# Sums of log decays by channel, made on TensorE for the first four units of an RWKV-7 and MLP kernel

## The chip, the cores and the metric

The kernel runs on one core of one Trainium2 chip. The metric is the device time of one execution in microseconds (us). A profiled execution has a time of its own, and its trace gives the span from the first to the last instruction; the time shown for the kernel is the median of several executions without profile.

## The reference

The program is an RWKV-7 attention block (batch 4, 8 heads, 768 steps, head width 40) followed by an MLP with a sigmoid-approximated GELU (3072 tokens, 320 to 2048 to 320). Everything is fp32.

```python
for t in range(S):                                   # S = 768
    y[:, :, t] = einsum('bhd,bhde->bhe', r_t, state)
    Sa = einsum('bhde,bhe->bhd', state, a_t)
    state = state * w_t[:, :, None, :] - einsum('bhd,bhe->bhde', Sa, b_t) + einsum('bhd,bhe->bhde', v_t, k_t)
x = y.transpose(0, 2, 1, 3).reshape(B * S, H * D)
h = x @ w_in
out = (h / (1 + exp(-1.702 * h))) @ w_out
```

The decay `w` lies between 0.85 and 0.95, per batch, head, step and channel. A blocked form of the recurrence needs products of `w` over steps, that is exponentials of sums of `log w`.

## The kernel before, in words

**Units.** The 768 steps are cut into 12 chunks of 64 steps. A unit is one chunk of two of the four batch entries, so there are 24 units, numbered i = 2c + p for chunk c and pair of batch entries p. Units of one pair follow each other in c, because the state is handed on. An MLP chunk c can start when units 2c and 2c+1 are finished.

**One unit.** `decay(i)` makes decay factors, `prep(i)` multiplies a, b, k by them and makes score matrices (`ps_A`, `ps_RV`), `inverse(i)` inverts triangular 64 x 64 systems by an iteration of five levels, and `solve(i)` makes the output and the next state. One level is: matmuls (`ps_level`), a copy of the result (`W`, line 651), a subtraction from two times the identity (`E`, line 653), a 32 x 32 block transposition (`ES`, line 615) and a masked spread of it (`EX`, line 620 on ScalarE, 622 on VectorE or GpSimd), which the next level's matmuls need. The unit's result `x` (line 814) is written to DRAM and read back transposed as `xT` (lines 824 and 828), for the MLP.

**The decay factors.** Two forms are needed.
- By time: steps on the partitions, channels on the free axis. `logw` (128 x 320, 160 KB, from `in_w`) is loaded, its logarithm taken in place (line 478), and `by_time` multiplies it by the constant matrix `incl` of 0, 1 and -1 on TensorE (`ps_cum`), which gives running sums measured from the middle of the chunk (MID = 32). `G` is their exponential (line 514).
- By channel: channels on the partitions, steps on the free axis. This is a second copy of `w`, laid out by the host: `wc` (128 x 528, 264 KB, from `in_wc`). Its logarithm is taken (line 477), and two scans on VectorE (lines 485 and 486) make the running sums, backwards from the middle for the first 32 steps and forwards for the others. `FT` (line 506) and `GT` (line 507), each 128 x 512, are their exponentials with plus and minus sign; `wch` (lines 509 and 510) holds the chunk's end values.

`FT` and `GT` scale a, k and b: the products `ak<-ak,FT` (line 541), `b<-b,GT` (543) and `ak<-ak,GT` (546) stand at the head of every unit's chain.

**Order.** Nothing in the program's text orders the engines. Each piece of work is a task in `Plan`, with a rank, a cost for every engine that may run it, what it reads and writes, how many buffers its outputs have, and if it uses PSUM, one of four pairs of banks. `Plan.order` runs a greedy list schedule with these costs: whenever an engine is free, it takes the able task of lowest rank. The order found is then emitted, and at run time each engine works through its own list and waits on semaphores. So any change of a task's cost can change the order of everything behind it. A task whose `engines` names several (for instance `EX`: POOL, DVE or ACT) goes to whichever is free first in that plan. DMA tasks stand in SyncE's list, and all DMAs are issued from SyncE's queue. The tasks that concern the change are

```python
def load_w(i):
    for name, of, src, n in (("wc", wc_of, wc_d, 528), ("logw", logw_of, w_d, DM)):
        plan.add(-2 if i == 2 else 10 * i - 30, {"SP": 350.0}, ...)
```

`logarithm(i)` and `decay(i)`. The functions `prep`, `inverse` and `solve` of a unit follow from its rank.

**The weights.** `w_in` and `w_out` arrive as eight pieces of 128 x 1280 64-bit numbers (1280 KB each). Each piece is turned into fp32 in `weight(n, ...)`: one ScalarE instruction (line 408) and five on VectorE (lines 412, 416, 417, 420 and 424; the sum of line 424 finishes the piece). Pieces 0 to 3 are `w_in`, which `ps_up` needs; pieces 4 to 7 are `w_out`, which `ps_down` needs. The MLP's matmuls have the highest rank numbers (10000 and up), so they fill TensorE where attention leaves it free.

**ScalarE's tables.** Logarithm and exponential share one table, the GELU has another. For the first four units (EARLY = 4) no GELU runs yet, and the exponentials stand without a table load before them.

Of the kernel before, what the change touches and what calls it, by code (L numbers as in the profile page):

```python
# [22 lines left out]
ALU = mybir.AluOpType  # L23
ACT = mybir.ActivationFunctionType
# [201 lines left out]
def rwkv7_gelu_quick(ctx: ExitStack, tc: tile.TileContext, time_d, v_d, w_d, wc_d, ak_d, b_d, rv_d, w_in, w_out, out):  # L226
    nc = tc.nc
    H, D, S = 8, 40, out.shape[0] // 4
    DM = H * D
    C = 64  # L230
    MID = C // 2
# [6 lines left out]
    LEVELS = 5  # L238
    WALK = "ebufbub"
    EARLY = 4  # L240
    ROUNDS, WINDOW, SHARE = 4, 5000.0, 1.0
    RANKS = [14, 16, 20, 24, 35, 37, 39, 41]
    HALF = [slice(0, 64), slice(64, 128)]
    BITS = (0, 1)
    QUARTERS = [(0, 0), (1, 1), (0, 1), (1, 0)]
# [7 lines left out]
    plan = Plan(dict(logw=3, wc=3, G=1, wch=3, wz=2, time=2, ak=2, b=2, rv=2, FT=3, GT=1, kh=2, bh=2, zr=2, rz=2,  # L253
                     A=1, B=1, RV=2, E0=2, W0=2, P21=2, W=2, E=2, ES=2, EX=2, T=2, Tc=1, QT=1, zraw=2, zT=1, M=2, x=1, xT=3, g=4, ob=1), 4)
    tiles, psums, drams = {}, {}, {}

    def single(name, shape):
        return const.tile(shape, FP32, tag=name, name=name)

    def buf(name, n, shape, dt=FP32):  # L260

        if (name, n) not in tiles:
            s = n % plan.slots[name]
            tiles[name, n] = work.tile(shape, dt, tag=f"{name}{s}", name=name)
        return tiles[name, n]

    def psum(t, name):
        if t.pair not in psums:
            psums[t.pair] = banks.tile([128, 2, 512], FP32, tag=f"pair{t.bank}", name=name)
        return psums[t.pair]  # L270

    def mm(o, lhsT, rhs, start):
        nc.tensor.matmul(o, lhsT, rhs, start=start, stop=True, skip_group_check=True)  # L273

    def head(e, f, b, u):
        return e + 2 * f + 4 * (b ^ u)


    def pe(*sets):

        return {"PE": sum(n * 2 * max(58.0, cols / 1.2 + 3) for n, cols in sets), "instr": sum(16 * n for n, _ in sets)}
# [13 lines left out]
    def of(e):  # L295
        return nc.gpsimd if e == "POOL" else nc.vector


    def several(name, shape):
        return [single(f"{name}{i}", shape) for i in range(plan.slots[name])]  # L300
# [18 lines left out]
    def select(t, compare, base, sign, fill):  # L319

        nc.gpsimd.affine_select(out=t, in_=t, compare_op=compare, fill=fill, base=base,
                                pattern=[[sign, t.shape[-1]]], channel_multiplier=-sign)


    incl = single("incl", [128, 64])
    nc.gpsimd.memset(incl, 1.0)
    for p in HALF:
        q = slice(p.start, p.start + MID)
        nc.gpsimd.memset(incl[q], 0.0)
        select(incl[q], ALU.is_ge, 0, 1, -1.0)  # L330
        select(incl[p.start + MID:p.stop], ALU.is_ge, -MID, 1, 0.0)

    starts = single("starts", [128, 8, 33])
    nc.gpsimd.memset(starts, 1.0)
# [106 lines left out]
    ak_of, b_of, rv_of = lambda i: ak_t[i % 2], lambda i: b_t[i % 2], lambda i: rv_t[i % 2]  # L441

    RV_of = lambda i: buf("RV", i, [128, 13, 8, 8])
    logw_of = lambda i: buf("logw", i, [128, DM])

    wc_of = lambda i: buf("wc", i, [128, 2, 8 * 33])

    def load_w(i):
        for name, of, src, n in (("wc", wc_of, wc_d, 528), ("logw", logw_of, w_d, DM)):
            plan.add(-2 if i == 2 else 10 * i - 30, {"SP": 350.0}, lambda t, of=of, src=src: nc.sync.dma_start(of(i), src[i]),  # L450
                     writes=[(name, i)], size=128 * n * 4)

# [14 lines left out]
    FT_of = lambda i: buf("FT", i, [128, 8, 64])  # L467
    GT_of = lambda i: buf("GT", i, [128, 8, 64])
    wch_of = lambda i: buf("wch", i, [128, 2, 8])
# [4 lines left out]

    def logarithm(i):
        def go(t):
            nc.scalar.activation(wc_of(i), wc_of(i), ACT.Ln)
            nc.scalar.activation(logw_of(i), logw_of(i), ACT.Ln)
        plan.add(10 * i - 30, {"ACT": 1080.0 + (1300.0 if i >= EARLY + 2 else 0.0)}, go,
                 reads=[("logw", i), ("wc", i)] + ([("exps", i - 2)] if i > 1 else []), writes=[("log", i)])  # L480

        def sums(t):

            wc, one = wc_of(i), starts.rearrange("p h t -> p (h t)")
            nc.vector.tensor_tensor_scan(wc[:, 0, ::-1], one, wc[:, 0, ::-1], 0.0, ALU.mult, ALU.subtract)
            nc.vector.tensor_tensor_scan(wc[:, 1], one, wc[:, 1], 0.0, ALU.mult, ALU.add)
        plan.add(10 * i - 12, {"DVE": 1400.0, "sbuf": True}, sums, reads=[("log", i)], uses=[("wc", i)], writes=[("sums", i)])

    def decay(i):
        T = lambda *names: [(n, i) for n in names]  # L490
        R = 10 * i - 9

        def by_time(t):
            ps, lw = psum(t, "ps_cum"), logw_of(i)
            for n in (1, 0):
                for b in BITS:
                    u = b ^ n
                    mm(ps[HALF[u], b, :160], incl[HALF[b]], lw[HALF[b], n * 160:(n + 1) * 160], True)
        plan.add(R, pe((1, 160)), by_time, reads=T("log"), uses=T("logw"), room=T("G"), writes=T("cum"), pair=("cum", i))

        def exp_channel(t):
            if i >= EARLY:
                nc.scalar.preload_act_table_set("natural_log_exp_and_others")
            sums = wc_of(i).rearrange("p n (h t) -> p n h t", t=33)
            by_half = lambda t: t.rearrange("p h (n t) -> p n h t", n=2)
            nc.scalar.activation(by_half(FT_of(i)), sums[:, :, :, :32], ACT.Exp)
            nc.scalar.activation(by_half(GT_of(i)), sums[:, :, :, 1:], ACT.Exp, scale=-1.0)

            nc.scalar.activation(wch_of(i)[:, 0], sums[:, 0, :, 0], ACT.Exp, scale=-1.0)
            nc.scalar.activation(wch_of(i)[:, 1], sums[:, 1, :, 32], ACT.Exp)  # L510

        plan.add(R, {"ACT": 1600.0 + (1300.0 if i >= EARLY else 0.0)}, exp_channel, reads=T("cum", "sums"), uses=T("wc"),
                 writes=T("FT", "GT", "wch"))
        plan.add(R, {"ACT": 460.0}, lambda t: nc.scalar.activation(G_of(i), psum(t, "")[:, :, :160], ACT.Exp, scale=-1.0),
                 reads=T("FT"), writes=T("G", "exps"), pair=("cum", i))
        if i >= 2:
            plan.add(R, {"DVE": 180.0, "POOL": 200.0}, lambda t: of(t.engine).tensor_mul(
                wz_of(i), wch_of(i)[:, 0], wch_of(i - 2)[:, 1]),
                     reads=T("wch") + [("wch", i - 2)], writes=T("wz"))
# [367 lines left out]
    for i in range(3):  # L887
        load_w(i)
    for i in range(2):
        logarithm(i)  # L890
# [3 lines left out]
    for i in range(NU):  # L894
        decay(i)
        if i + 3 < NU:
            load_w(i + 3)
        if i + 2 < NU:
            logarithm(i + 2)
        if i >= 2:  # L900
            load(i)
        prep(i)
        inverse(i)
        solve(i)
        if i % 2:
            mlp(i // 2)
# [88 lines left out]
```

## Time and profile before

| | before |
|---|---|
| median of 3 executions | 743.05 us (742.98 to 743.25) |
| the profiled execution's own time | 743.23 us |
| its span in the trace | 741.2 us (2.03 us lie outside it) |
| mean granted TensorE clock | 0.969 |
| busy: PE, PEld, VectorE (DVE), ScalarE (ACT), GpSimd (POOL) | 672.6, 539.6, 445.1, 372.8, 223.3 us |
| DMA traffic | 70.86 MB |

PE is TensorE's matmuls, PEld its weight loads, which lie beside them. The engines' busy shares are means over the whole span, and this kernel has two stages with different limits: at the start no MLP work is there, and from about 75 us on there is. A row of the profile names the line, the engine, the operation, and the tile written and the tiles read (`wc<-starts,wc`), with the number of instructions behind an x. All matmuls have line 273 or 272, that of the helper `mm`, and are told apart by their tiles. An fp32 matmul appears as two passes, each with its weight load. "issue" is time for which the trace shows no reason.

### The profile page before, as it was taken

The page shows a single profiled execution, that of the slowest core. Times are in us where ns is not written, and L with a number is a line of the kernel's source. Part 1 is how long each engine was busy: PE and PEld are TensorE (multiplying, and loading weights), DVE is VectorE, ACT ScalarE, POOL GpSimd, SP SyncE. Part 2 cuts the span into 40 slices and gives each one's busy share as a digit, 9 for nine tenths or more (in the row PEclk, how much of TensorE's full clock was granted, in tenths as well). Part 3 has the DMA queues.
Part 4 walks back from the last instruction along what each step waited for, and adds up shares of the span by engine and source line. Part 5 has one row for each costly group of instructions (what it writes and reads, how often), then busy time and mean ns, then how long its engine had stood idle before and what let it go on. Part 6 is the DMA issues. An engine that isn't in the chain of part 4 may idle for free.

```text
span 741.2 us, 43007 instructions
## 1 busy us (share of the span) xinstructions
PE 672.6 (91%) x19968; PEld 539.6 (73%) x19968; DVE 445.1 (60%) x783; ACT 372.8 (50%) x693; POOL 223.3 (30%) x279
## 2 busy tenths in 40 slices
PE   3464896898998999999999999999999999999997
PEld 2364674686776776988778889888678877987564
DVE  6889897876567556666766656666547556421000
ACT  4764664358447439545544544745845444342120
POOL 7554244242304331233332522322332433100000
PEclk9678997999999999999999999999999999999999
DMA  7964361242323332242332332341331220111000
GB/s 226 356 203 132 132 226 42 85 122 82 101 55 99 105 85 87 75 138 71 108 94 71 107 101 63 98 135 45 100 101 48 76 84 21 31 47 30 12 11 19
DMA packets 32434, 70.86 MB, mean 96 GB/s; under 512 B 5120, under 2 KB 14336, under 8 KB 31232
## 3 DMA queue, kind: packets, MB, share of 16 engines
q1 hardware_dynamic: 32256, 68.11, 30.1%
q8 instruction: 157, 2.57, 1.5%
q14 instruction: 21, 0.17, 0.1%
HBM read 60.23 MB, written 7.86 MB: 92 GB/s over the span
## 4 chain that ended last, share of the span: by engine, by line
PE 77%; ACT 10%; DVE 7%; DMA 2%; issue 2%; POOL 1%; DVEq 0%; ACTq 0%; POOLq 0%; SPq 0%
PE ps_down L273 27%; PE ps_up L273 23%; PE ps_level L273 7%; PE ps_y L273 4%; PE ps_B L273 4%; PE ps_X L273 2%; ACT L849 2%; ACT g L849 2%; PE ps_Q L273 1%; ACT EX L620 1%; PE ps_zT L273 1%; DVE ES L615 1%; PE ps_T L273 1%; PE ps_rz L273 1%; PE ps_N L273 1%
## 5 line engine op out<-in xcount | busy, mean ns | idle before, releaser
L273 PE MATMUL ps_up<-xT,w_sb 64*64 64x256 f32 x3840 | 250.0, 380 | 5.1 <-ACT g L849 4.4
L273 PE MATMUL ps_down<-w_sb,g 64*64 64x320 f32 x3072 | 241.6, 434 | 0.9 <-issue 0.5
L273 PEld LDWEIGHTS ps_up<-xT,w_sb 64*64 64x64 f32 x3840 | 150.2, 134 | 36.1 <-ACT g L849 5.6
L273 PEld LDWEIGHTS ps_down<-w_sb,g 64*64 64x64 f32 x3072 | 128.3, 134 | 48.9 <-issue 3.1
L273 PEld LDWEIGHTS ps_level<-W,EX 64*64 64x64 f32 x3840 | 85.1, 143 | 45.8 <-ACT EX L620 14.6
L273 PE MATMUL ps_level<-W,EX 64*64 64x64 f32 (+1 forms) x3840 | 87.3, 228 | 27.6 <-ACT EX L620 11.6
L620 ACT ACTIVATE EX<-ES,quads 128x256 f32<-128x256 f32 x124 | 56.2, 501 | 60.4 <-DVE ES L615 60.1
L651 ACT COPY W<-ps_level 128x512 f32<-128x512 f32 x66 | 38.5, 584 | 80.4 <-PE ps_level L273 76.6
L549 POOL TENSOR_TENSOR kh<-time,G 128x320 f32<-128x320 f32 x24 | 23.8, 991 | 161.2 <-issue 100.8
L849 ACT ACTIVATE g<-ps_up 128x1024 f32<-128x1024 f32 x48 | 49.1, 1024 | 43.5 <-PE ps_up L273 43.2
L653 DVE TENSOR_TENSOR E<-two,ps_level 128x256 f32<-128x256 f32 x96 | 39.7, 414 | 42.5 <-ACT W L651 41.9
L615 DVE STREAM_TRANSPOSE ES<-E 128x256 f32<-128x256 f32 x120 | 53.0, 443 | 5.9
L622 POOL TENSOR_TENSOR EX<-ES,quads 128x512 f32<-128x512 f32 x26 | 39.7, 1527 | 51.1 <-DVE ES L615 35.6
L875 DVE TENSOR_TENSOR ob<-ob,ps_down 128x320 f32<-128x320 f32 x24 | 11.6, 484 | 63.5 <-ACT ob L873 63.1
L610 POOL TENSOR_TENSOR W<-two,E 128x256 f32<-128x256 f32 x23 | 18.0, 783 | 91.6 <-DVE E L604 84.0
L752 ACT COPY B<-ps_B 128x416 f32<-128x416 f32 x42 | 21.1, 504 | 45.9 <-PE ps_B L273 45.8
L541 POOL TENSOR_TENSOR ak<-ak,FT 128x512 f32<-128x512 f32 x21 | 29.7, 1416 | 39.1 <-DMA ak<-in_ak 18.4
L814 POOL TENSOR_TENSOR x<-zr,FT 128x128 f32<-128x128 f32 x80 | 40.9, 540 | 1.7 <-ACT zr L806 1.7
L273 PE MATMUL ps_y<-RV,kh 64*64 64x104 f32 x768 | 36.0, 250 | 1.3 <-DVE M L768 1.1
L273 PE MATMUL ps_y<-M,bh 64*64 64x104 f32 x768 | 35.8, 249 | 0.4 <-issue 0.4
L768 DVE TENSOR_TENSOR M<-ps_X,later 128x832 f32<-128x832 f32 x24 | 24.5, 1019 | 17.3 <-PE ps_X L273 17.1
L651 DVE COPY W<-ps_level 128x512 f32<-128x512 f32 x30 | 20.6, 687 | 22.2 <-PE ps_level L273 22.2
(122 smaller groups left out, 1075.7 us busy)
## 6 DMA issues: line engine op xcount, KB each, us to landing
ak<-in_ak SPq DMA_DIRECT2D x48, 160.0 KB
time<-in_time SPq DMA_DIRECT2D x24, 320.0 KB
rv<-in_rv SPq DMA_DIRECT2D x48, 160.0 KB
xT<-x_dram SPq DMA_DIRECT2D x48, 160.0 KB
wc<-in_wc SPq DMA_DIRECT2D x24, 264.0 KB
extra<-in_w_out SPq DMA_DIRECT2D x4, 1280.0 KB
logw<-in_w SPq DMA_DIRECT2D x24, 160.0 KB
b<-in_b SPq DMA_DIRECT2D x48, 80.0 KB
```

The lines of the kernel that those rows point to most:

```text
L273: nc.tensor.matmul(o, lhsT, rhs, start=start, stop=True, skip_group_check=True)
L541: plan.add(R, {"DVE": 690.0, "POOL": 1270.0, "sbuf": True}, lambda t: of(t.engine).tensor_mul(ahT(), ahT(), FT_of(i)), reads=T("ak", "FT") ...
L549: plan.add(R + 4, {"POOL": 870.0, "DVE": 490.0, "sbuf": True}, lambda t, n=n, dst=dst: of(t.engine).tensor_mul(dst(i)[:, :, :D], by_head(t ...
L615: plan.add(rank, dve(256), lambda t: nc.vector.transpose(ES(n), source(t)), writes=[key("ES", n, 6)], **reads)
L620: nc.scalar.activation(dst[:, :, h], ES(n), ACT.Copy, scale=quads[:, h, :1])
L622: of(t.engine).tensor_mul(dst, ES(n).unsqueeze(2).to_broadcast([128, 8, 2, 32]), quads.unsqueeze(1).to_broadcast([128, 8, 2, 32]))
L651: plan.add(rank, any2(512), lambda t: copy(t.engine)(tiles_of(W(n + 1)), blocks(psum(t, ""), 64)), writes=[key("W", n + 1, 5)], pair=pair)
L653: plan.add(rank, dve(256), lambda t: nc.vector.tensor_sub(tiles_of(E(n + 1)), every(two32, [128, 2, 4, 32]), blocks(psum(t, ""), 64)[:, :, ...
L752: plan.add(R, any2(416), lambda t: copy(t.engine)(dst(), psum(t, "")[:, :, :208]), writes=[("Bv", i)] if x and c > 0 else T("B"), pair=(na ...
L768: plan.add(R + 1, dve(832), lambda t: nc.vector.tensor_tensor(M_of(i).rearrange("p (j b) n -> p b j n", b=2), psum(t, "")[:, :, :416].rear ...
L814: of(t.engine).tensor_mul(x[:, b ^ u, b], both(i)[:, at, :64], FT_of(i)[:, at])
L849: plan.add(-45, act(1024), lambda t: nc.scalar.activation(g_of(c * NQ + q).rearrange("p m r n -> p r m n"), psum(t, "").rearrange("p r (m ...
```

## The change

For units 0 to 3 (`BY_PE = 4`) the sums by channel are no longer made from the second copy of `w`. The by-time logarithm `logw` is used as the stationary operand and a 0, 1, -1 matrix as the moving one, so that the product has channels on its partitions and steps on its free axis. The moving matrix is `edges`, `incl` with one more column, so that the 65 columns hold the exclusive and the inclusive running sums together; `incl` becomes `edges[:, 1:]`. `logw` gets three fixed buffers with 24 further columns of zero, since a weight load takes 64 columns and a head has 40. `FT` and `GT` are then exponentials of the PSUM result, in two instructions each (one for each bank of the pair), and `wch` in four instead of two. The load of `wc`, its logarithm and its two scans are left out for these units. Units 4 to 23 work as before.

```diff
+    BY_PE = 4
...
-    incl = single("incl", [128, 64])
-    nc.gpsimd.memset(incl, 1.0)
+    edges = single("edges", [128, 65])
+    nc.gpsimd.memset(edges, 1.0)
     for p in HALF:
         q = slice(p.start, p.start + MID)
-        nc.gpsimd.memset(incl[q], 0.0)
-        select(incl[q], ALU.is_ge, 0, 1, -1.0)
-        select(incl[p.start + MID:p.stop], ALU.is_ge, -MID, 1, 0.0)
+        nc.gpsimd.memset(edges[q], 0.0)
+        select(edges[q], ALU.is_gt, 0, 1, -1.0)
+        select(edges[p.start + MID:p.stop], ALU.is_gt, -MID, 1, 0.0)
+    incl = edges[:, 1:]
+    logw_t = several("logw", [128, DM + 24])
+    for t in logw_t:
+        nc.gpsimd.memset(t[:, DM:], 0.0)
...
-    logw_of = lambda i: buf("logw", i, [128, DM])
+    logw_of = lambda i: logw_t[i % 3][:, :DM]
...
-        for name, of, src, n in (("wc", wc_of, wc_d, 528), ("logw", logw_of, w_d, DM)):
+        for name, of, src, n in (("wc", wc_of, wc_d, 528), ("logw", logw_of, w_d, DM))[i < BY_PE:]:
...
         def go(t):
-            nc.scalar.activation(wc_of(i), wc_of(i), ACT.Ln)
+            if i >= BY_PE:
+                nc.scalar.activation(wc_of(i), wc_of(i), ACT.Ln)
             nc.scalar.activation(logw_of(i), logw_of(i), ACT.Ln)
-        plan.add(10 * i - 30, {"ACT": 1080.0 + (1300.0 if i >= EARLY + 2 else 0.0)}, go,
+        plan.add(10 * i - 30, {"ACT": (1080.0 if i >= BY_PE else 450.0) + (1300.0 if i >= EARLY + 2 else 0.0)}, go,
...
-        plan.add(10 * i - 12, {"DVE": 1400.0, "sbuf": True}, sums, reads=[("log", i)], uses=[("wc", i)], writes=[("sums", i)])
+        if i >= BY_PE:
+            plan.add(10 * i - 12, {"DVE": 1400.0, "sbuf": True}, sums, reads=[("log", i)], uses=[("wc", i)], writes=[("sums", i)])
...
+        def by_channel(t):
+            ps = psum(t, "ps_cumc")
+            for u, f in product(BITS, BITS):
+                for b, e in QUARTERS:
+                    o, h = (2 * u + f) * 65, head(e, f, b, u) * D
+                    mm(ps[HALF[e], b, o:o + 65], logw_t[i % 3][HALF[b], h:h + 64], edges[HALF[b]], o == 0)
+
+        def exp_of_product(t):
+            sums = psum(t, "")[:, :, :260].rearrange("p b (j t) -> p b j t", t=65)
+            for b in BITS:
+                of_b = lambda x: x.rearrange("p (u b f) t -> p b u f t", u=2, b=2)[:, b]
+                got = sums[:, b].rearrange("p (u f) t -> p u f t", u=2)
+                nc.scalar.activation(of_b(FT_of(i)), got[:, :, :, :64], ACT.Exp)
+                nc.scalar.activation(of_b(GT_of(i)), got[:, :, :, 1:], ACT.Exp, scale=-1.0)
+            ends = wch_of(i).rearrange("p n (u b f) -> p n b u f", u=2, b=2)
+            for n in BITS:
+                for b in BITS:
+                    nc.scalar.activation(ends[:, n, b], sums[:, b, :, 64 * n].rearrange("p (u f) -> p u f", u=2), ACT.Exp, scale=2.0 * n - 1.0)
+
+        if i < BY_PE:
+            plan.add(R, pe((4, 65)), by_channel, reads=T("log"), uses=T("logw"), room=T("FT", "GT"), pair=("cumc", i))
...
-        plan.add(R, {"ACT": 1600.0 + (1300.0 if i >= EARLY else 0.0)}, exp_channel, reads=T("cum", "sums"), uses=T("wc"),
-                 writes=T("FT", "GT", "wch"))
+        if i < BY_PE:
+            plan.add(R, {"ACT": 2400.0}, exp_of_product, reads=T("cum"), writes=T("FT", "GT", "wch"), pair=("cumc", i))
+        else:
+            plan.add(R, {"ACT": 1600.0 + (1300.0 if i >= EARLY else 0.0)}, exp_channel, reads=T("cum", "sums"), uses=T("wc"),
+                     writes=T("FT", "GT", "wch"))
```

More of the change, by code (lines that the diff above doesn't have):

```diff
@@ L476, in go @@
         def go(t):
-            nc.scalar.activation(wc_of(i), wc_of(i), ACT.Ln)
+            if i >= BY_PE:
+                nc.scalar.activation(wc_of(i), wc_of(i), ACT.Ln)
             nc.scalar.activation(logw_of(i), logw_of(i), ACT.Ln)
-        plan.add(10 * i - 30, {"ACT": 1080.0 + (1300.0 if i >= EARLY + 2 else 0.0)}, go,
-                 reads=[("logw", i), ("wc", i)] + ([("exps", i - 2)] if i > 1 else []), writes=[("log", i)])
+        plan.add(10 * i - 30, {"ACT": (1080.0 if i >= BY_PE else 450.0) + (1300.0 if i >= EARLY + 2 else 0.0)}, go,
+                 reads=[("logw", i)] + ([("wc", i)] if i >= BY_PE else []) + ([("exps", i - 2)] if i > 1 else []), writes=[("log", i)])
         def sums(t):
```

## The prediction

> **What bounds the kernel now.** I read the page's busy table first, then the engines' busy time by stage, then the chain of waits in the first 75 us, then the timeline between 95 and 140 us. The page's first part:
>
> ```profile
> PE 672.6 (91%) x19968; PEld 539.6 (73%) x19968; DVE 445.1 (60%) x783; ACT 372.8 (50%) x693; POOL 223.3 (30%) x279
> ```
>
> TensorE is busy 91% of the span, so the kernel's end is its work plus its idle time, and the question is where the idle 68.6 us (741.2 - 672.6) are. The stages (columns: stretch, its length, then busy us of each engine, granted clock, DMA share, GB/s):
>
> ```profile
> 0.00:20.00 20.00, 6.82 (x146) 5.23 (x146) 13.10 (x23) 10.36 (x24) 15.39 (x47) 1.00 0.80 232
> 20.00:40.00 20.00, 9.17 (x346) 8.12 (x350) 18.04 (x27) 14.76 (x29) 11.45 (x10) 0.64 0.90 342
> 40.00:60.00 20.00, 12.91 (x510) 11.29 (x504) 17.43 (x28) 12.12 (x28) 10.12 (x9) 0.84 0.56 182
> 60.00:73.30 13.30, 6.40 (x236) 5.74 (x240) 13.09 (x19) 5.73 (x14) 5.54 (x5) 0.75 0.47 139
> 73.30:100.00 26.70, 23.85 (x720) 19.16 (x714) 22.62 (x31) 18.24 (x29) 7.79 (x6) 0.93 0.39 125
> 100.00:125.00 25.00, 17.05 (x460) 11.72 (x456) 22.70 (x32) 13.87 (x26) 14.49 (x12) 0.86 0.48 163
> ```
>
> Until 73.3 us, where the first `ps_up` starts, TensorE idles 38.0 us; from there to 125 us another 10.8. After 150 us it idles little (7.9 us to 300, 4.1 from 300 to 700). So the end moves with what happens before about 140 us. There VectorE is busy about 90% from 20 us on, and before 20 us DMA is. The chain of waits of the first stage (start, us, what):
>
> ```profile
> 3.13 5.22 DMA ak<-in_ak
> 8.37 5.56 DMA logw<-in_w
> 13.95 6.58 DMA rv<-in_rv
> 20.57 0.63 PE ps_RV L273 x27
> ...
> 52.53 1.37 DVE w_sb L424
> 53.90 1.29 DVE wc L485
> 55.20 0.60 DVE wc L486
> ```
>
> The reader sees three transfers end to end until 20.5 us, then VectorE instructions, among them unit 3's two scans, which this change removes. Last, the weights' join in the timeline, and what stands beside it:
>
> ```profile
> 121.91 1.45 DVE L424 TENSOR_TENSOR w_sb<-w_sb,extra 128x1280 f32<-128x1280 f32 x1
> 123.41 4.54 PE L273 MATMUL ps_down<-w_sb,g 64*64 64x320 f32 x32
> 135.32 1.45 DVE L424 TENSOR_TENSOR w_sb<-w_sb,extra 128x1280 f32<-128x1280 f32 x1
> ```
>
> Piece 6 of the weights is finished at 123.4 us and TensorE takes it up at once; piece 7 ends at 136.8. VectorE's queue, not TensorE, sets this stage too.
>
> [...] the trace shows 342 with DMA 90% busy at 20 to 40 us, [...] and bytes left out there save time. [...] the instruction of line 416 took 0.79 us with GpSimd idle and 1.71 us beside it, so work moved to GpSimd can cost VectorE time.
>
> **The change part by part.** The sum is made against the profiled execution, 743.23 us (741.2 of span and 2.0 around it), which is 0.18 above the median 743.05.
>
> *Loads.* Four loads of 264 KB go. In the order of the changed program, three of them stood ahead of unit 1's `rv`: 3 x 270,336 = 811 KB. At 342 GB/s this is 2.4 us, at the first stage's 232 GB/s 3.5. The third transfer of the chain ends 2.4 us earlier; **-2.4**. SP's queue loses four issues of 0.33 to 0.43 us, not on the path, as it waits for transfers. The load of unit 4's `wc` moves ahead of the first weight piece (another 270 KB, 0.8 us); the piece's DMA still stands 541 KB earlier than before, so this costs nothing.
>
> *Scans.* Eight scans of 0.68 us median, 6.1 us as run (3.4 + 2.7). The four of units 0 and 1 ran while VectorE waited for loads and are worth nothing beyond the loads; unit 2's two (16.16 to 17.45) delayed unit 0's `E` of 17.37, but `ps_level` of unit 0 stands behind `ps_RV` of unit 1, which waits for the `rv` load, so nothing again. Unit 3's stand on the chain from 53.90 to 55.80: **-1.9**.
>
> *ScalarE.* Per unit, the logarithm of `wc` goes (0.64, 0.55 from start to start). `FT`, `GT`, `wch` took 1.27 us from start to start until `G` (7.20 to 8.47). Now there are four instructions of 256 elements from PSUM: the nearest row, the copy of `ps_N`, takes 0.37, 0.28 from start to start; and four small ones at 0.105: 1.54 us. [...] Net -0.2 to -0.3 us per unit, on an engine that is busy 12 to 15 of 20 us: 0. Against this, `FT` is complete with the third instruction instead of the first, 0.3 us later after its start, `GT` 0.1; for unit 0 the start moves from 7.20 to about 6.1 (`logw` logarithm 3.74 to 4.2, `ps_cum` 0.8, `ps_cumc` 1.1 like the cold `ps_A`), so both still come earlier.
>
> *TensorE.* Per unit 32 passes of 65 columns; 32 passes of 64 (`ps_RV`) take 0.64 warm, 1.13 cold: 2.6 us in all. They lie before the first `ps_up`, where TensorE idles 38.0 us: 0, and 2.6 if that cover were gone. A queue behind them: `ps_RV` or `ps_level` of another unit waits up to 0.7 to 1.1 us, and `ps_cumc` holds one of four pairs of banks. Bounds -0.5 to +2.6; I take 0.
>
> *GpSimd.* Three memsets of 24 columns, 0.11 each like that of `zT`, and one column more in `edges`: it fills constants until 12.9 us anyway. 0.
>
> *Order.* This is the largest unknown, since the planner reorders everything. In the built programs, the matmuls ahead of the first `ps_up` are worth 25.4 us before and 31.2 after at warm durations (64 columns 20 ns a pass, 104: 22, 160: 34, 256: 54, 320: 68); less the added 2.6 this is 3.2 us more of old work done there, up to -3.2 if the first `ps_up` doesn't move. On the other side, VectorE's instructions at undisturbed durations, from unit 0's first `EX` to piece 7's join, sum to 93.4 us before and 99.7 after: scans are down from six to four there, but eight x multiplications instead of four, two `EX` and two `Tc` and `zT` copies more were moved to it; some 2.5 of the 6.3 is later units' work done sooner. The two have opposite signs and like size; I take 0, with -3.5 to +6.
>
> Sum: -2.4 - 1.9 = -4.3, so 743.2 - 4.3 = **738.9 us**.
>
> **The rivals.** *A larger gain.* If the early loads shift the first `ps_up` by 4.3 us and the extra old work stays done, the gain is up to 7.5: 735.7. For it speaks that TensorE is near saturation from there on; against it that it then waits for pieces 6 and 7, whose DVE work has not shrunk.
>
> *Nothing to be measured.* VectorE's time saved is filled by moved work, so that piece 7 joins at about 136.8 - 2.4 + 4 = 138; TensorE has by then done about 2.6 us more old work (73.8 against 71.2 at warm durations) and the net is about -1: 742. The change of order speaks for it.
>
> *Slower.* The same place priced in full: the moved 6.3 us of VectorE work, stretched by GpSimd as in the trace (93.9 us busy from 20 to 125 us and, at the next stage's share of 0.80, some 9.4 to 136.8, against 93.4 nominal: 1.11), is 7.0; less 2.4 for loads, piece 7 joins 4.6 later, and less the 2.6 of work done ahead the end is 2.0 later: 745.2. It decides once piece 7 joins after 139.4. The planner also gives GpSimd more `EX` and `T` early (14 against 7 by the fourth `wz`), which speaks for it; that VectorE idles 10% of the stage speaks against.
>
> *The change doesn't do what it says:* the built program has none of the eight scans and four loads left, so this could only be bytes fetched elsewhere; hardly.
>
> **How the numbers follow.** Two tenths of a per cent, 1.5 us, is about what a measurement of this kernel can tell from no change. Chances: the forecast (736.5 to 741.5) 0.45, the larger gain 0.21, nothing 0.18, slower 0.15, no such change 0.01. Faster by over 0.2%: the first two and a little of the third's edge, 0.69; within: 0.16; slower 0.15. The range leaves out the best part of the larger gain and the slowest: 733.5 to 744.6.
>
> **What would show it.** In the profile after: `ps_RV` of unit 1 starts near 18 us instead of 20.57; DMA traffic 69.8 MB; VectorE has no scans before 80 us; the first `ps_up` comes at 68 to 72 us; piece 7 joins at 134 to 138. It is wrong if `rv` lands no earlier, if the first `ps_up` comes after 75, or if TensorE's idle time to 150 us isn't less than 52 by at least 4.

## The result, and the profile after

The changed kernel takes 739.75 us (median of 12 executions, 736.91 to 742.58), the kernel before 743.38 beside it (12 executions, 742.82 to 748.62). The ratio on record is 0.9926, with a 95% interval of 0.9902 to 0.9950: faster by 0.7%, or 5.5 us. It is not the ratio of the two medians, which are 3.6 us apart, so the size of the gain is known to some 2 us only. The profiled execution lies at the upper end of its group, 741.96 us with a span of 740.3, so its trace shows where time moved better than how much of it was saved.

The rows of the page that answer to the one shown before: busy us with share of the span and number of instructions of each engine, then the DMA packets.

```profile
PE 679.0 (92%) x20096; PEld 560.7 (76%) x20096; DVE 445.9 (60%) x795; ACT 343.8 (46%) x666; POOL 214.5 (29%) x279
DMA packets 31860, 69.80 MB, mean 94 GB/s; under 512 B 5056, under 2 KB 14272, under 8 KB 30656
```

Bytes fell as computed, from 70.86 to 69.80 MB. The row to stop at is ScalarE's (ACT): it lost 29 us of busy time, 372.8 to 343.8, while the four removed logarithms are worth some 2.6 (0.64 or 0.65 each in the trace before). The largest part, 20.5 us, is loads of function tables (`ACT_TABLE_LOAD`: ScalarE changes between the table of the gelu and that of logarithm and exponential; in the trace before, one load at 0.80 us is all that stands ahead of the logarithms and exponentials of the first 80 us, and the next comes at 80.65 us, right ahead of the first gelu), as the groups of ScalarE show (number of loads, busy us, mean ns, idle before). First before, then after:

```profile
L849 ACT ACT_TABLE_LOAD x21 | 26.9, 1283 | 0.4
L503 ACT ACT_TABLE_LOAD x20 | 25.7, 1283 | 0.4
L477 ACT ACT_TABLE_LOAD x6 | 7.7, 1283 | 0.1
L514 ACT ACT_TABLE_LOAD x5 | 6.4, 1283 | 0.1
```

```profile
L533 ACT ACT_TABLE_LOAD x20 | 25.7, 1283 | 0.3
L882 ACT ACT_TABLE_LOAD x12 | 15.4, 1283 | 0.2
L547 ACT ACT_TABLE_LOAD x2 | 2.6, 1283 | 0.0
L483 ACT ACT_TABLE_LOAD x2 | 2.6, 1283 | 0.0
```

With one at the start, 53 loads became 37. Nothing in the diff asks for this: the planner's new order puts gelus (`g`) beside gelus and exponentials beside exponentials.

The early stages of the changed kernel (columns as in the stages shown before):

```profile
0.00:20.00 20.00, 9.12 (x272) 8.34 (x272) 10.31 (x18) 8.62 (x29) 15.12 (x51) 0.92 0.78 242
...
73.30:100.00 26.70, 23.79 (x664) 20.04 (x664) 21.82 (x31) 16.80 (x27) 8.47 (x9) 0.78 0.47 148
```

VectorE is less busy than before (10.31 against 13.10 and 21.82 against 22.62 us). TensorE is busy 2.3 us longer in the first stage and about as long in the other, but there at a lower granted clock (0.78 against 0.93, and 664 passes against 720), so the same busy time is less work. The chain of the first stage; unit 1's `zr` and `x` and the first `ps_up` in the timeline, and piece 7's join:

```profile
11.45 6.38 DMA rv<-in_rv
17.95 1.31 PE ps_RV L274 x23
```

```profile
68.92 0.59 ACT L839 COPY zr<-ps_y 128x512 f32<-128x512 f32 x1
...
69.59 3.96 POOL L847 TENSOR_TENSOR x<-zr,FT 128x128 f32<-128x128 f32 x4 [0.18 <-ACT zr L839]
...
81.32 2.93 PE L274 MATMUL ps_up<-xT,w_sb 64*64 64x256 f32 x24 [0.62 <-ACT B L785]
...
142.57 1.47 DVE L429 TENSOR_TENSOR w_sb<-w_sb,extra 128x1280 f32<-128x1280 f32 x1
```

The same `zr` and `x` before, and the first `ps_up`:

```profile
62.32 0.58 ACT L806 COPY zr<-ps_y 128x512 f32<-128x512 f32 x1
...
64.55 1.62 DVE L814 TENSOR_TENSOR x<-zr,FT 128x128 f32<-128x128 f32 x4
...
73.02 3.68 PE L273 MATMUL ps_up<-xT,w_sb 64*64 64x256 f32 x32
```

`ps_RV` of unit 1 comes 2.6 us earlier (20.57 before). After that the early stages are not ahead: `ps_up` starts 8 us later than before, and piece 7 is finished at 144.04 instead of 136.77 us. The kernel is faster all the same, so its gain must lie elsewhere. These are the rows of the stretch from 150 to 300 us, before and after:

```profile
150.00:300.00 150.00, 142.08 (x4432) 111.75 (x4428) 95.09 (x172) 89.44 (x159) 41.88 (x56) 1.00 0.31 91
```

```profile
150.00:300.00 150.00, 145.75 (x4556) 126.45 (x4557) 100.30 (x188) 72.97 (x139) 50.44 (x57) 1.00 0.33 94
```

At the same granted clock of 1.00 TensorE is busy 3.7 us longer and issues 124 more passes, and ScalarE is busy 16.5 us less. TensorE's listed waits in this stretch before come to 7.7 us. The rows that end with a gelu (`g`) or with the exponential `G` are these (us in all, times, longest):

```profile
PE ps_up L273 <- ACT g L849: 2.9, 3, 1.5
PE ps_level L273 <- ACT G L514: 0.9, 1, 0.9
PE ps_B L273 <- ACT g L849: 0.9, 1, 0.9
...
PE ps_N L273 <- ACT g L849: 0.5, 1, 0.5
```

After, the list for this stretch has no such wait; these are all its rows:

```profile
PE ps_up L274 <- DVE RV L605: 1.5, 1, 1.5
PE ps_down L274 <- issue: 1.3, 2, 0.7
PE ps_rz L274 <- ACT zT L752: 1.1, 1, 1.1
PE ps_down L274 <- DVE QT L716: 0.3, 1, 0.3
```

One such place in the chain of waits before shows how they come about (start, us, what):

```profile
166.23 0.91 ACT EX L620 x2
...
167.16 1.28 ACT L503
...
168.46 0.63 ACT FT L506
169.09 0.52 ACT GT L507
169.61 0.11 ACT wch L509
169.72 0.10 ACT wch L510
...
169.84 1.28 ACT L849
...
171.13 1.02 ACT g L849
172.16 0.27 ACT P L607
...
172.44 1.28 ACT L514
...
173.73 0.45 ACT G L514
...
174.22 0.69 PE ps_level L273 x32
```

ScalarE's list runs for 8 us without a break, three table loads of 1.28 us in it (the pieces without a tile, L503, L849, L514), and TensorE has used up what it could do meanwhile: it waits 1.5 us for the gelu to release its banks to `ps_up`, and 0.9 for `G`.

### The profile page after: what moved, and what is told of

It is laid out like the page before. It is cut to its first block, busy times and chain, and to the rows that moved or that the text cites. A ratio compares the mean times of both kernels' runs of the same rounds, so it can differ in the third digit from the quotient of the medians.

```text
span 740.3 us, 43272 instructions
## 1 busy us (share of the span) xinstructions
PE 679.0 (92%) x20096; PEld 560.7 (76%) x20096; DVE 445.9 (60%) x795; ACT 343.8 (46%) x666; POOL 214.5 (29%) x279
## 2 busy tenths in 40 slices
DMA packets 31860, 69.80 MB, mean 94 GB/s; under 512 B 5056, under 2 KB 14272, under 8 KB 30656
## 4 chain that ended last, share of the span: by engine, by line
PE 77%; DVE 7%; ACT 5%; DMA 5%; issue 2%; POOL 2%; SPq 2%; DVEq 0%; POOLq 0%; ACTq 0%
PE ps_down L274 25%; PE ps_up L274 25%; PE ps_level L274 7%; PE ps_y L274 4%; PE ps_B L274 4%; PE ps_X L274 2%; PE ps_T L274 2%; PE ps_Q L274 2%; DMA ak<-in_ak 1%; PE ps_rz L274 1%; DVE ES L648 1%; PE ps_N L274 1%; PE ps_RV L274 1%; PE ps_A L274 1%; DMA extra<-in_w_out 1%
## 5 line engine op out<-in xcount | busy, mean ns | idle before, releaser
L274 PE MATMUL ps_down<-w_sb,g 64*64 64x320 f32 x3072 | 246.6, 436 | 4.9 <-DVE w_sb L429 2.5
L274 PEld LDWEIGHTS ps_up<-xT,w_sb 64*64 64x64 f32 x3840 | 152.7, 134 | 32.0 <-DVE RV L605 1.6
L274 PEld LDWEIGHTS ps_down<-w_sb,g 64*64 64x64 f32 x3072 | 135.6, 135 | 50.3 <-issue 7.6
L653 ACT ACTIVATE EX<-ES,quads 128x256 f32<-128x256 f32 x120 | 54.5, 501 | 59.7 <-DVE ES L648 57.5
L684 ACT COPY W<-ps_level 128x512 f32<-128x512 f32 x67 | 39.3, 586 | 71.5 <-PE ps_level L274 71.2
L655 POOL TENSOR_TENSOR EX<-ES,quads 128x512 f32<-128x512 f32 x26 | 37.7, 1449 | 80.3 <-DVE ES L648 57.6
L582 POOL TENSOR_TENSOR kh<-time,G 128x320 f32<-128x320 f32 x22 | 19.7, 894 | 123.9 <-PE ps_y L274 72.1
L847 POOL TENSOR_TENSOR x<-zr,FT 128x128 f32<-128x128 f32 x80 | 42.7, 563 | 5.4 <-DVE zr L837 3.4
L643 POOL TENSOR_TENSOR W<-two,E 128x256 f32<-128x256 f32 x22 | 16.1, 731 | 95.5 <-DVE E L637 95.5
L574 POOL TENSOR_TENSOR ak<-ak,FT 128x512 f32<-128x512 f32 x18 | 26.9, 1496 | 26.2 <-DMA ak<-in_ak 20.9
L655 POOL TENSOR_TENSOR T<-ES,quads 128x512 f32<-128x512 f32 x10 | 12.8, 1278 | 71.1 <-DVE ES L648 66.4
```

The source lines that it names most:

```text
L574: plan.add(R, {"DVE": 690.0, "POOL": 1270.0, "sbuf": True}, lambda t: of(t.engine).tensor_mul(ahT(), ahT(), FT_of(i)), reads=T("ak", "FT") ...
L582: plan.add(R + 4, {"POOL": 870.0, "DVE": 490.0, "sbuf": True}, lambda t, n=n, dst=dst: of(t.engine).tensor_mul(dst(i)[:, :, :D], by_head(t ...
L653: nc.scalar.activation(dst[:, :, h], ES(n), ACT.Copy, scale=quads[:, h, :1])
L655: of(t.engine).tensor_mul(dst, ES(n).unsqueeze(2).to_broadcast([128, 8, 2, 32]), quads.unsqueeze(1).to_broadcast([128, 8, 2, 32]))
L684: plan.add(rank, any2(512), lambda t: copy(t.engine)(tiles_of(W(n + 1)), blocks(psum(t, ""), 64)), writes=[key("W", n + 1, 5)], pair=pair)
L847: of(t.engine).tensor_mul(x[:, b ^ u, b], both(i)[:, at, :64], FT_of(i)[:, at])
```

## The experiments

Two theories. **Resources**: the removed loads, logarithms and scans give the time. **Order**: the planner's other lists give it, by taking TensorE's waits behind ScalarE away. Each kernel was measured together with the kernel before. The first four of the following form one group, measured side by side on one chip, and so do the next four and the last four. Times are compared within a group, ratios across groups.

**The changed kernel again**, with no edit.

> The changed kernel once more, for a second profile. Its executions so far spread from 736.9 to 742.6 us, those of the kernel before from 742.8 to 744.8. If the spread comes from the clock that TensorE is granted in the first 150 us, then two profiles of the same program differ there, in stages of clock under 1, and agree to 0.5 us after 200 us. If it comes from later, they part after 200 us. Median expected 739 to 740.5.

Measured: 735.28 us (before 742.20), ratio 0.9911 [0.9880, 0.9943]. By the measure "behind" of the table below, its profile is 2.2 us ahead of the first one at 150 us, and 3.9 at 300. So the two part before 150 us, where the granted clocks differed (0.71 in the first and 0.73 in the second up to 80 us), but they part further after 150 us, where both were at 1.00: the expectation about the clock came half true.

**The new sums in the old order.** The lists of the kernel before, word for word; `ps_cumc` is issued with `ps_cum` and lies in free columns of its banks.

```diff
+            if i < BY_PE:
+                for u, f in product(BITS, BITS):
+                    for b, e in QUARTERS:
+                        o, h = 160 + (2 * u + f) * 65, head(e, f, b, u) * D
+                        mm(ps[HALF[e], b, o:o + 65], logw_t[i % 3][HALF[b], h:h + 64], edges[HALF[b]], False)
```

> The mechanism without the new order: every engine's list stands as in the kernel before, but for units 0 to 3 the loads of wc, their logarithm and the scans are left out, and the sums by channel are made by TensorE right behind ps_cum, in free columns of the same pair of banks. Theory of resources (freed loads and scans in the first 60 us are the gain): 737 to 740, as the changed kernel. Theory of order (the gain is made by the planner's other order, after 200 us): 742 to 744, as before.

Measured: 742.38 us, ratio 1.0013 [0.9989, 1.0037]. The resources alone, in the old order, bring no gain that can be seen (by the interval, 0.8 us at most). Their first effects are there: `ps_RV` of unit 1 ends at 18.16 us instead of 21.26, and the first `ps_up` comes at 71.80 us instead of 73.02.

**The new order with the old sums.** The lists of the changed kernel; at the place of `ps_cumc` the two scans are issued, and the loads and logarithms of `wc` are back (in space of their own).

```diff
+            wc, one = wc_first(i), starts.rearrange("p h t -> p (h t)")
+            nc.vector.tensor_tensor_scan(wc[:, 0, ::-1], one, wc[:, 0, ::-1], 0.0, ALU.mult, ALU.subtract)
+            nc.vector.tensor_tensor_scan(wc[:, 1], one, wc[:, 1], 0.0, ALU.mult, ALU.add)
```

> The new order without the mechanism: every engine's list stands as in the changed kernel, but units 0 to 3 load wc again (just ahead of logw), take its logarithm and make the sums by two scans, which stand in VectorE's list where ps_cumc stood in TensorE's. Theory of resources: 743 to 748, as before or slower, for the loads (2.4 us) and scans (1.9) are back. Theory of order: 739 to 742, as the changed kernel or little above.

Measured: 739.58 us, ratio 0.9964 [0.9947, 0.9982]. The order alone gains 2.7 us. The 4.3 us from here to the changed kernel of the same group (735.28) are what the new sums are worth in this order.

**The changed kernel with the four loads kept**, into space that nothing reads at that time.

```diff
+ ... [nc.sync.dma_start(wc_first(i).rearrange("p n t -> p (n t)"), wc_d[i])] if i < BY_PE else [], ...
```

> The changed kernel with the four loads of wc of 264 KB still issued, just ahead of logw, into space that is free at the time; nobody reads them. Theory of resources, as in the prediction: unit 1's rv lands 2.4 us later (20.4 instead of 17.9) and the time grows by 2 to 3 us. Theory of order: rv lands later all the same, but the end moves by less than 1 us, as the shift is lost again before 150 us.

Measured: 738.00 us, ratio 0.9943 [0.9919, 0.9967]. `ps_RV` of unit 1 begins at 19.55 us instead of 17.95. The time lies between the two others: by the medians, the loads account for 2.7 of the 4.3 us and the scans and logarithms for 1.6. The intervals overlap, and against the third result for the changed kernel below (0.9933) the loads account for only 0.7 us, so the split isn't settled. In both kernels the kept `wc` lies in the space of later weight pieces, whose loads may have waited for it; that was not separated.

Next, the order's gain was to be tied to ScalarE, by edits of its list alone.

**Fewer table loads in the old order.** Only ScalarE's list of the kernel before is regrouped: `G`, and often the logarithms of the unit two later, directly behind `FT`, `GT` and `wch`.

```diff
+            exp_channel_alone(t)
+            nc.scalar.activation(G_of(i), psums["cum", i][:, :, :160], ACT.Exp, scale=-1.0)
+            if i + 2 < NU and i + 2 not in taken and all(loaded.get((n, i + 2), 1e9) + 6000 <= t.start for n in ("wc", "logw")):
+                log_go[i + 2](t)
...
```

> The kernel before, with its lists of instructions on TensorE, VectorE, GpSimd and the queues as they are. Only ScalarE's list is changed: the exponential of a unit that reads TensorE's sums by time (G), and in most units the logarithm of the unit two later, are issued right behind the unit's other exponentials, where before other work and gelus lay between. That takes the loads of function tables from 53 to the changed kernel's 37, 16 loads or 16 x 1.28 = 20.5 us of ScalarE's time, with loads, logarithms and scans all kept. The theory that the new order gains by fewer table loads expects what the changed order with the old sums gained, 2 to 5 us: a ratio of 0.993 to 0.997. The theory that the gain lies in where the planner puts TensorE's work, or in the resources freed, expects no change, 0.999 to 1.001; a loss is possible where a G that is issued early delays a copy that TensorE waits for.

Measured: 761.01 us, ratio 1.0253 [1.0224, 1.0283]. This is a clear miss. One cause is the edit's own, logarithms that now wait for their load at the head of ScalarE's list (17.8 us in all, one of them 12.8; in the kernel before such waits take 5.3 us):

```profile
ACT wc L481 <- DMA wc<-in_wc: 17.8, 3, 12.8
```

**More table loads in the new order.** In the changed kernel, ahead of eight of the first 18 gelus the exponential's table is loaded, and so the gelu's again.

```diff
+    AWAY = (2, 5, 6, 9, 10, 13, 14, 17)
...
+            plan.add(-45, act(1024), lambda t: (c * NQ + q in AWAY and nc.scalar.preload_act_table_set("natural_log_exp_and_others"), nc.scalar.activation)[1](
```

> The changed kernel with its lists as they are, but for eight gelus of the first 18, ahead of each of which ScalarE loads the exponential's table and then the gelu's again: 16 loads more, 37 to 53, which is the count of the kernel before. The theory of the table loads expects 3 to 6 us of the gain back, a ratio to before of 0.996 to 1.000. The theory that TensorE's order or the freed resources make the gain expects the changed kernel's own ratio, 0.990 to 0.993, within 1 us.

Measured: 745.84 us, ratio 1.0045 [1.0023, 1.0066], against 737.56 for the changed kernel of the same group: 8.3 us, more than either theory expected. TensorE's, VectorE's and GpSimd's lists are unchanged, so the cost comes from ScalarE alone. The chain of waits in one of these places, and TensorE's waits from 150 to 300 us:

```profile
176.97 0.59 ACT W L684
...
177.57 1.28 ACT L884
...
178.86 1.28 ACT L884
...
180.16 1.03 ACT g L884
...
181.23 0.74 PE ps_level L274 x32
```

```profile
PE ps_level L274 <- ACT g L884: 3.5, 3, 1.9
```

The waits behind gelus are back.

**Fewer table loads and new sums in the old order** (the two edits together).

> Before's order with the new way of making the sums (the second kernel of the first call), and with ScalarE's list regrouped as in the kernel with fewer table loads: 37 loads in place of 53. The first call gave the new sums in the old order 1.0013 with 53 loads. The theory of the table loads, with the freed resources worth something once ScalarE no longer holds TensorE up, expects 0.989 to 0.994, like the changed kernel. The theory that the planner's order of TensorE's work matters of itself expects 0.999 to 1.002.

Measured: 758.72 us, ratio 1.0209 [1.0172, 1.0245]. It misses both expectations. It shares the first regrouping's fault, and tells little more.

**The changed kernel a third time.**

> The changed kernel again, on the chip of these comparisons, so that the three others have it beside them: 0.988 to 0.994 by its first two results.

Measured: 737.56 us (before 741.96), ratio 0.9933 [0.9907, 0.9959].

**Fewer table loads, from unit 4 on.** The regrouping without its fault: ScalarE's waits for loads of `wc` are 5.0 us here, against the 5.3 of the kernel before.

```diff
+            if i < EARLY:
+                return
             nc.scalar.activation(G_of(i), psums["cum", i][:, :, :160], ACT.Exp, scale=-1.0)
```

> The regrouping of ScalarE's list once more, from the fifth unit on only, where the second load of the decays has landed at least 16 us before the place to which the logarithm moves (in the first try three logarithms waited 17.8 us for that load, one of them 12.8 us, and held ScalarE's list up ahead of the MLP). All other lists are as before, loads, logarithms and scans stay, and there are 37 table loads in place of 53. Sixteen added loads cost the changed kernel 8 us, so the theory of the table loads expects 3 to 8 us less than before, a ratio of 0.989 to 0.996. The rival, that it matters which wait of TensorE a load lies in and not how many there are, expects 0.997 to 1.004 here, since work is also moved ahead of copies that TensorE waits for.

Measured: 749.60 us (before 745.26), ratio 1.0053 [1.0032, 1.0075]. With 37 table loads, the changed kernel's number, it is slower than before with 53. So the theory that counts table loads falls; the time is even a little above the rival's range. Its waits from 150 to 300 us say why:

```profile
PE ps_up L273 <- ACT g L862: 4.7, 2, 2.6
PE ps_N L273 <- ACT g L862: 1.7, 1, 1.7
PE ps_B L273 <- ACT g L862: 0.9, 1, 0.9
```

The moved logarithms and `G` now stand in one block ahead of a gelu, and TensorE waits longer for that gelu than it did before.

**The lists redrawn.** In the kernel before, one planning figure is changed; instructions and sums stay, all lists come out otherwise.

```diff
-        plan.add(10 * i - 12, {"DVE": 1400.0, "sbuf": True}, sums, ...)
+        plan.add(10 * i - 12, {"DVE": 1300.0, "sbuf": True}, sums, ...)
```

> The kernel before with one number of its planning changed: a unit's scans are planned at 1300 ns and not 1400. The program computes by the same instructions, but the planner's lists come out otherwise all along, and with 36 table loads. The theory of the table loads expects 735 to 740, a ratio of 0.991 to 0.997. The rival, that any redrawing of the lists scatters the time whatever the table loads, expects a ratio anywhere from 0.99 to 1.02.

Measured: 737.49 us, ratio 0.9876 [0.9834, 0.9918]. The time is as the theory of the table loads expected, the ratio below both expectations. A figure in the plan, with nothing removed, gains as much as the change under study or more: the intervals overlap (0.9880 to 0.9959 over the three results of the changed kernel), and the two were never measured in one group. TensorE's stretch from 150 to 300 us:

```profile
150.00:300.00 150.00, 148.10 (x4666) 129.56 (x4661) 101.17 (x181) 76.21 (x148) 43.74 (x52) 1.00 0.31 90
```

The same figure at 1380:

> The same with 1380 ns in place of 1400: lists redrawn, with 55 table loads. The theory of the table loads expects 742 to 745, a ratio of 0.999 to 1.004. The rival expects a ratio anywhere from 0.99 to 1.02, with no relation to the table loads.

Measured: 743.16 us, ratio 0.9976 [0.9953, 0.9998], in time as the theory of the table loads expected, in ratio a little below, and within the rival's range.

**The new sums in the redrawn lists**: the edit of the second kernel with 1300 in place of 1400.

> The lists of the redrawing with 36 table loads, with the new way of making the sums put into them (the sums by channel issued with the sums by time, no second load, no scans for the first four units). If new sums are worth what they were in the changed kernel's order, 4 us, this is 0.992 to 0.996 of the kernel with the same lists and old sums; if they are worth what they were in the old order, nothing, it is that kernel's time within 1.5 us.

Measured: 738.63 us, ratio 0.9880 [0.9840, 0.9921], that is 1.1 us above the same lists with the old sums. So no gain of the new sums is seen here either, but with six executions of each kernel one of up to some 4 us isn't excluded (the two intervals, taken together, leave the difference of the ratios uncertain by about 0.006).

**All together.** For each profile: the table loads; the time that TensorE waited behind a gelu (the sum of its waits that end with `g`), over the run and from 150 to 300 us; and how far TensorE is behind at 150 and 300 us. "Behind" is the time minus the matmul passes done so far at the warm durations used in the prediction (such as 54 ns for a pass of 256 columns: at 165.04 us of the trace before, 16 passes of `ps_up` took 0.86 us from start to start), without the passes of the new sums. Only its differences count, and the three profiles of the changed kernel, which are one program, differ by 4.9 us at 150 us and by 2.3 us in the last column.

| kernel | ratio | table loads | waits behind `g`: run, 150-300 | behind at 150, 300 | change |
|---|---|---|---|---|---|
| before | 1 | 53 | 9.6, 4.3 | 66.3, 66.7 | +0.4 |
| changed | 0.9926 | 37 | 2.5, 0 | 70.1, 66.0 | -4.1 |
| changed, again | 0.9911 | 37 | 1.7, 0 | 67.9, 62.1 | -5.8 |
| changed, third | 0.9933 | 37 | 1.6, 0 | 65.2, 58.8 | -6.4 |
| old order, new sums | 1.0013 | 53 | 9.4, 4.2 | 63.8, 65.8 | +2.0 |
| new order, old sums | 0.9964 | 37 | 1.9, 0 | 69.8, 63.9 | -5.9 |
| loads kept | 0.9943 | 37 | 1.9, 0 | 71.2, 65.1 | -6.1 |
| fewer loads | 1.0253 | 37 | 15.4, 5.8 | 80.5, 84.1 | +3.6 |
| more loads | 1.0045 | 53 | 11.0, 3.5 | 70.1, 69.9 | -0.2 |
| fewer loads, new sums | 1.0209 | 37 | 15.2, 7.6 | 76.5, 78.5 | +2.0 |
| fewer loads, late | 1.0053 | 37 | 15.3, 7.3 | 65.5, 68.9 | +3.4 |
| redrawn, 1300 | 0.9876 | 36 | 0.8, 0 | 65.2, 57.6 | -7.6 |
| redrawn, 1380 | 0.9976 | 55 | 9.4, 3.9 | 62.7, 65.7 | +3.0 |
| redrawn, new sums | 0.9880 | 36 | 0.8, 0 | 69.0, 64.4 | -4.6 |

There are two groups. Where no wait behind a gelu is left from 150 to 300 us, TensorE makes up 4.1 to 7.6 us there; with 3.5 to 7.6 us of such waits it makes up nothing or loses. The ratios divide in the same way, 0.9876 to 0.9964 against 0.9976 and more (the two nearest have overlapping intervals), and the number of table loads doesn't divide them. That ScalarE's list alone can make the difference is shown by two edits of nothing else: added loads brought 9.4 us of these waits over the run and cost 8.3 us (against the changed kernel of the same group), and moved work brought 5.7 us of them (4.8, if the 0.9 us of waits behind `G` that went are set off) and cost 0.53%, 4.0 us, against before. The sizes agree with the waits as the way in which it acts. The waits behind gelus don't price a whole order, though. The new order with the old sums has 7.7 us less of them than before and gains 2.7; all the waits that TensorE's profile lists fell by only 2.0 us there (61.1 against 63.1), since those of the first 80 us grew from 37.7 to 40.2. Nor does that total decide: with the new sums in the old order it is 58.1, and nothing is gained. That the new order's gain has no other part isn't shown: its lists on the other engines were never run with ScalarE's old one.

## Why the prediction was right in its total and wrong in its place

The prediction gave 738.9 us in a range of 733.5 to 744.6, and faster as the likeliest case; measured were 739.75 and 0.9926. Step by step:

- **Loads and scans, -4.3.** In the changed kernel's order the new sums measured -4.3 (735.28 against 739.58 in one group); by the ratios of the two other results, 0.9926 and 0.9933 against 0.9964, it is -2.8 and -2.3. So sign and rough size are right there, and most of it is there early: at 80 us the three profiles of the changed kernel are 49.6 to 51.5 us behind, the one with old sums 53.9. But in the old order, in which the sum was made, at most 0.8 us of it arrives (1.0013 [0.9989, 1.0037]), and in the redrawn lists none is seen (0.9880 against 0.9876). Why these two orders don't keep the gain is open: the profiles with the new sums differ there from those with the old by 0.9 to 6.8 us in "behind" at 150 and 300 us, which is no more than profiles of one program do (4.9 and 7.2).
- **`rv` earlier by 2.4.** `ps_RV` of unit 1 starts at 17.95 us, 2.6 earlier (16.61 and 16.34 in the other two profiles). Right or better, and the bytes are right.
- **ScalarE's exponentials, 0.** Right in effect. For unit 0 the eight instructions take 1.29 us from the start of the first to `G`, against 1.54 in the sum: the four small ones start 0.05 us apart, where 0.105 was taken. From the trace the net per unit was an estimate of 1.54 - 1.27 - 0.55 = -0.28 us; the -0.2 beside it wasn't shown by any trace.
- **TensorE's added matmuls, hidden.** `ps_cumc` of unit 0 took 1.1 us, at 4.7 us, where TensorE idled anyway. Its size was right; that it is free in every order isn't shown. Its 32 weight loads are of 64 x 64, as all 20096 in that trace are; that one of a head's 40 columns would not do isn't shown either.
- **First `ps_up` at 68 to 72 us.** Wrong: 81.32 (78.86 and 78.18 in the other two profiles), all after the 75 us that the prediction named as a sign of being wrong. The step assumed that the gain of loads and scans moves it as it stands. But `ps_up` needs units 0 and 1, and the new lists finish unit 0's `x` 5.4 us earlier (53.3 against 58.7) but unit 1's `zr`, from which its `x` is made, 6.6 us later (69.51 against 62.90). The new lists also give that `x` to GpSimd, where it takes 2.3 us longer (3.96 against 1.62); as it waits 1.6 us less to begin, it ends 7.4 us later. The last thing that `ps_up` waits for is then the copy `B`. Where unit 1's chain lost the 6.6 us was not followed. In the old order `ps_up` came at 71.80, inside the forecast. Nor does a late `ps_up` decide the end: in the redrawn lists with 1300 it comes at 81.50.
- **Piece 7 at 134 to 138, and 139.4 as the point from which the change loses.** It came at 144.04 in the first profile, 140.9 in the second and 138.9 in the third, and all three executions belong to a kernel that is faster. The "slower" rival had its mechanism, later weights, but not its price: a lateness of the join is not paid in full.
- **TensorE's idle time to 150 us less by at least 4.** It fell from 52.0 to 46.6 us, yet TensorE had issued fewer passes of the old work by then (3015 against 3050, without the 128 of the new sums): it was busy longer at a granted clock of 0.80, where it had been 0.85. The test passed without meaning what it was to mean.
- **Order, 0 with -3.5 to +6.** This is the step that failed. The order alone is worth -2.7 us (0.9964 [0.9947, 0.9982]), inside its bounds, but it was priced only up to piece 7's join, and up to there it brings nothing: the new order with the old sums is 3.5 us further behind at 150 us than before, which lies within the scatter of such profiles. A gain of 5.9 comes from 150 to 300 us, of which the prediction said that TensorE idles little (7.9 us). Those 7.9 us were the place: 5.9 of the 7.7 us of waits there ended with ScalarE, 4.3 of them with a gelu, and the page's ACT share of 10% in the chain that ended last pointed at it.
- **Two readings of the lines.** The "slower" rival says that GpSimd gets more `EX` and `T` early, 14 against 7 by the fourth `wz`. The traces give these counts if only `wz` on GpSimd is counted; in the new lists three run on VectorE, so GpSimd's fourth starts at 204.07 us, against 112.37 before. Up to 140 us GpSimd starts 9 of them against 10 before. And the 0.79 us of line 416 was not taken with GpSimd idle (an `EX` began there 0.22 us after it); with nothing beside it the line took 0.82 and 0.85 us (at 86.68 and 97.67 us), and beside GpSimd's `ak` and `EX` 1.71 (at 112.98), so the point that work on GpSimd can cost VectorE time stands on these.

So the total came out right in part by luck, by two things that happen to agree in sum: the order gave -2.7 where 0 was taken, and the new sums between -2.3 and -4.3 where -4.3 was taken, though in the order for which the sum was made they gave nothing to be seen.

## What to carry to other kernels

Where a planner writes the lists, price a change twice: once in the old order and once as what the new lists do to every stage, and run a redrawn list without the change as a control. Here such a control moved the time by as much as the change did or more. On an engine that works through its list in order and holds other engines' buffers, as ScalarE here, look at what stands in one block ahead of the instruction that releases them. Here 16 table loads less (20.5 us) with work moved into such blocks cost 4.0 us, and 16 more in such blocks 8.3 us.

## What was not expected of the hardware

- A load of ScalarE's function table took 1283 ns in every profile of this case. Regrouping that removed 16 of them (20.5 us of ScalarE's time) made the kernel slower (1.0053), and adding 16 cost 8.3 us: the time went with TensorE's waits behind gelus (15.3 us against 9.6 before in the one, 11.0 against 1.6 for the changed kernel in the other), not with the number of loads.
- Executions of one program on one core scatter more than the three times shown before suggested (742.98 to 743.25): the kernel before had 738.36 to 747.94 in one group, and the changed kernel's profiles differ by 4.9 us in "behind" at 150 us. The further behind, the lower the granted clock up to there (0.80, 0.81 and 0.84 for 70.1, 67.9 and 65.2 us behind), but they differ by 7.2 us at 300, after a stretch at 1.00 in all three. What differs between such executions was not settled.
- The best ratio to before is that of the redrawn lists without the change, 0.9876 [0.9834, 0.9918], though its interval overlaps those of the changed kernel.
